# First groups transposed on TensorE, one softmax for both ends, and a new planner cost, in a dynamic convolution with Fourier mixing and an MLP

## The chip, the cores and the metric

The kernel runs on one NeuronCore of a Trainium2 chip. The metric is the time of one execution on the device, in microseconds (us). Five engines work beside each other, each in its own order: PE (TensorE, matrix products), DVE (VectorE), ACT (ScalarE), POOL (GpSimd) and SP (SyncE, which here issues all transfers). An instruction waits at the head of its engine until what it needs is there, and everything behind it on that engine waits with it.

## The reference

The input x has 8 batches of 4224 positions with 192 channels; weight_gen has for each position 8 heads with 7 taps.

```python
w = softmax(weight_gen, axis=-1)                      # with 1e-9 in the sum
x_pad = zeros of 6 positions in front of x
c[b, s, head] = sum_k w[b, s, head, k] * x_pad[b, s + k, head]   # 24 channels a head
u = c + real(fft(fft(c, axis=1), axis=2))
un = (u - mean(u)) / sqrt(var(u) + 1e-6)              # over the channels
out = u + relu(un @ w_ch1) @ w_ch2                    # 192 -> 768 -> 192
```

## The kernel before

The 4224 positions of a batch lie as 128 partitions by 33 rows; the host puts them in an order in which the transform along the sequence splits in a DFT of 128 and one of 33. Each batch goes through these stages.

- **conv**: softmax of the taps (`softmax_taps`, L503 to L515: load, maximum, subtraction, Exp on ACT, sum, reciprocal), weights made of it (wp, L604), products of x with the weights by chunk c of four rows, 0 to 8 (DVE at L673 `pr<-x_sb,wp`, POOL at L671, in batch 0 some on ACT at L641), and their sums: on PE by a matmul with the identity for some chunks of batch 0 (L679, L650), on POOL else (L683 `u<-u,pr`). Batches 0 and 1 make the softmax in three parts, rows 0 to 4, rows 29 to 32 and the middle.
- **transform**: POOL folds mirrored rows (sm, L697 and L699), PE makes the DFT of 128 (pg, L704), DVE gathers (gt, L711, L714), the result goes to DRAM (g_d) and comes back in another order (g, L739), PE makes the DFT of 33 (pp, L749), ACT copies it to pq (L753 to L763).
- **mix**, by group g of four rows, 0 to 8: PE makes the transform along the channels (eo, L778), ACT copies one half (ot, L783), DVE adds it to u (L784 to L788).
- **norm**: mean and variance (groups 0 to 2 of batch 0, the `QUICK` ones, by DVE at L812; else by ACT at L817, L819), the root on ACT (L821), the normalized un (ACT, L830), which is split into two fp16 parts hl (cast on ACT at L838, remainder at L839 and L841 on DVE for quick groups, on POOL else), and a DMA transpose of hl to ht (L847).
- **mlp**, numbered 0 to 71 over all batches: 30 fp16 matmuls `ph<-ht` (L872) with the two parts of w1, relu (ACT, with DVE at L883), then `po<-hh` (L895, f32 for the first 7 groups, three fp16 terms afterwards), addition to u (L900) and the output.

w1 and w2 arrive as wide words and are turned to f32 by seven DVE steps a part (L430 to L441, prep_w1, prep_w2), then split (split_f32).

The code lists these streams in a rough order (`add`, `queue`, `held`), and `plan()` then sets the order of every engine for the whole program: it walks the instructions with a cost for each (`cost()`), a time between engines (`HOP`), the Exp and Sqrt table load on ACT, and the buffers that come free, and keeps the best of several walks. Tiles of one tag share buffers in turn: "ph" has 3 banks of PSUM, "po" has 2, ht has 3 buffers in SBUF. `held(ins)` puts the instructions written in it behind `ins`.

`keep_warm` (L726) issues matmuls whose result nobody reads, so that PE isn't idle: 20 behind the last pg of batch 0 (warm_pp), 12 on hl_0 (warm_hl), 12 ahead of the MLP of group 1 (`late_warm`).

## Time and profile before

| what | before |
|---|---|
| runs | 1120.19, 1113.48, 1117.24 us; median 1117.24 |
| profiled execution | 1118.23 us, its span 1116.5 us |
| granted TensorE clock, mean | 0.989 of full |
| PE busy | 1072.5 us, 96% of the span |
| DVE, POOL, ACT busy | 964.1, 875.8, 820.4 us |
| moved by DMA | 128.71 MB, mean 115 GB/s |

Times in the profile run from the start of the span. A row of the timeline has the start, the length, the engine, the line of the kernel, the operation, and what it writes and reads; a bracket at the end is the idle time of the engine just before, and what ended it. Rows of matmuls count passes: an f32 matmul is two records. A DMA row on SPq is the issue alone.

### The profile page before, as it was taken

The page shows a single profiled execution, that of the slowest core. Times are in us where ns is not written, and L with a number is a line of the kernel's source. Part 1 is how long each engine was busy: PE and PEld are TensorE (multiplying, and loading weights), DVE is VectorE, ACT ScalarE, POOL GpSimd, SP SyncE. Part 2 cuts the span into 40 slices and gives each one's busy share as a digit, 9 for nine tenths or more (in the row PEclk, how much of TensorE's full clock was granted, in tenths as well). Part 3 has the DMA queues.
Part 4 walks back from the last instruction along what each step waited for, and adds up shares of the span by engine and source line. Part 5 has one row for each costly group of instructions (what it writes and reads, how often), then busy time and mean ns, then how long its engine had stood idle before and what let it go on. Part 6 is the DMA issues. An engine that isn't in the chain of part 4 may idle for free.

```text
span 1116.5 us, 23468 instructions
## 1 busy us (share of the span) xinstructions
PE 1072.5 (96%) x8476; PEld 822.3 (74%) x8476; DVE 964.1 (86%) x1773; ACT 820.4 (73%) x2415; POOL 875.8 (78%) x759
## 2 busy tenths in 40 slices
PE   5885999999989999999999999999999999999998
PEld 3464687887768877777778877787778777886777
DVE  7988998889979999999989999999989998355543
ACT  4665666769866887878797878778787878689832
POOL 5979799799959999599969999599969999111200
PEclk9997999999999999999999999999999999999999
DMA  9354136514464246624454337614543322613221
GB/s 319 122 154 113 36 115 188 140 40 135 124 171 105 79 121 196 146 66 121 114 169 104 93 108 212 145 48 124 128 136 103 72 61 71 146 44 75 72 48 47
DMA packets 156500, 128.71 MB, mean 115 GB/s; under 512 B 108571, under 2 KB 133088, under 8 KB 156384
## 3 DMA queue, kind: packets, MB, share of 16 engines
q1 hardware_dynamic: 156384, 127.21, 42.6%
q8 instruction: 67, 1.10, 0.4%
q14 instruction: 49, 0.40, 0.1%
HBM read 61.46 MB, written 39.37 MB: 90 GB/s over the span
## 4 chain that ended last, share of the span: by engine, by line
PE 66%; POOL 10%; DVE 9%; issue 5%; DMA 3%; ACT 2%; SPq 0%; DVEq 0%; ACTq 0%; POOLq 0%
PE ph L872 28%; PE po L895 26%; POOL u L683 8%; PE pp L749 5%; PE eo L778 4%; DVE pr L673 3%; PE pg L704 2%; DMA g<-g_d 1%; DVE hh L883 1%; POOL sm L697 1%; PE pa L679 1%; DMA ht<-hl 1%; DMA g_d<-gt 1%; ACT un L830 1%; DVE u L673 1%
## 5 line engine op out<-in xcount | busy, mean ns | idle before, releaser
L683 POOL TENSOR_TENSOR u<-u,pr 128x768 f32<-128x768 f32 (+1 forms) x396 | 654.9, 1675 | 20.3 <-DVE pr L673 9.5
L895 PE MATMUL po<-w2h,hh 128*128 128x192 f16 x2832 | 421.9, 246 | 0.1
L895 PEld LDWEIGHTS <-hh 128*128 128x128 f16 x4248 | 364.8, 98 | 70.0 <-issue 0.6
L872 PE MATMUL ph<-ht,w1h 128*128 128x512 f16 (+1 forms) x1296 | 400.9, 363 | 6.8 <-DMA ht<-hl 3.9
L673 DVE TENSOR_TENSOR pr<-x_sb,wp 128x768 f32<-128x768 f32 (+1 forms) x415 | 356.2, 880 | 21.7 <-POOL u L683 19.3
L895 PE MATMUL po<-w2l,hh 128*128 128x192 f16 x1416 | 348.3, 246 | 0.0
L883 DVE SCALAR_TENSOR_TENSOR hh<-ph,hh 128x512 f16<-128x512 f32 (+1 forms) x390 | 247.9, 638 | 80.2 <-ACT hh L882 79.6
L872 PE MATMUL ph<-ht,w1l 128*128 128x512 f16 (+1 forms) x864 | 311.4, 363 | 0.0
L882 ACT ACTIVATE hh<-ph 128x512 f16<-128x512 f32 (+1 forms) x390 | 214.8, 551 | 121.5 <-PE ph L872 94.4
L872 PEld LDWEIGHTS <-w1h 128*128 128x128 f16 x1296 | 126.3, 99 | 88.3 <-DMA ht<-hl 3.5
L830 ACT ACTIVATE un<-u,rs 128x192 f32<-128x192 f32 x264 | 127.6, 536 | 31.5 <-POOL rs L828 23.3
L839 POOL TENSOR_TENSOR hl<-un,hl 128x512 f16<-128x512 f32 (+1 forms) x69 | 74.3, 1076 | 70.0 <-ACT hl L838 36.1
L872 PEld LDWEIGHTS <-w1l 128*128 128x128 f16 x864 | 85.7, 99 | 44.6 <-issue 3.0
L819 ACT ACTIVATE junk<-u,st 128x192 f16<-128x192 f32 x252 | 113.6, 451 | 4.1
L817 ACT ACTIVATE junk<-u 128x192 f16<-128x192 f32 x252 | 90.6, 360 | 22.7 <-DVE u L788 19.1
L778 PE MATMUL eo<-cs_sb,pq 97*128 97x97 f32 x544 | 88.1, 271 | 2.1 <-DVE u L788 1.9
L778 PEld LDWEIGHTS eo<-cs_sb,pq 97*128 97x128 f32 x544 | 81.9, 191 | 11.1 <-issue 2.1
L900 DVE SCALAR_TENSOR_TENSOR u<-po,isc,u 128x384 f32<-128x384 f32 (+1 forms) x122 | 73.0, 598 | 10.8 <-PE po L895 10.6
L828 POOL TENSOR_TENSOR rs<-st,rs 128x4 f32<-128x4 f32 (+1 forms) x69 | 13.8, 202 | 80.9 <-DVE rs L822 76.8
L697 POOL TENSOR_TENSOR sm<-u 128x382 f32<-128x382 f32 x64 | 64.5, 1008 | 4.0 <-ACT u L692 4.0
L753 ACT COPY pq<-pp 97x204 f32<-97x204 f32 (+1 forms) x96 | 46.4, 484 | 26.3 <-PE pp L749 21.7
L895 PE MATMUL po<-w2f,hh 128*128 128x192 f32 x336 | 64.3, 328 | 0.0
(108 smaller groups left out, 1291.2 us busy)
## 6 DMA issues: line engine op xcount, KB each, us to landing
out_dram<-u SPq DMA_DIRECT2D x64, 384.0 KB
x_sb<-in_x_dram SPq DMA_DIRECT2D x48, 384.0 KB
g<-g_d SPq DMA_DIRECT2D x40, 336.0 KB
x_sb<-in_x_dram SPq DMA_DIRECT2D x8, 864.0 KB
g_d<-gt SPq DMA_DIRECT2D x32, 195.0 KB
g_d<-gt SPq DMA_DIRECT2D x32, 189.0 KB
w<-in_weight_gen_dram SPq DMA_DIRECT2D x6, 924.0 KB
x_sb<-in_x_dram SPq DMA_DIRECT2D x8, 672.0 KB
```

The lines of the kernel that those rows point to most:

```text
L673: last_product[b] = nc.vector.tensor_tensor(out=dst, in0=rows, in1=wk, op=ALU.mult)
L683: adder.tensor_tensor(out=u, in0=u, in1=pr, op=ALU.add)
L697: nc.gpsimd.tensor_tensor(out=sm[:, :, 1:D], in0=u[:, 0:2, 1:D], in1=u[:, 3:1:-1, D - 1:0:-1], op=ALU.add)
L778: nc.tensor.matmul(eo[:, e, j, :], lhsT=pq[0:DH, e, r, r:r + P], rhs=cs_sb[:, e, :], start=True, stop=True)
L817: nc.scalar.activation(junk, uv[:, t, :], AF.Identity, scale=-1.0 / D, accum_out=st[:, t, 0:1])
L819: nc.scalar.activation(junk, uv[:, t, :], AF.Square, bias=st[:, t, 0:1], accum_out=st[:, t, 1:2])
L830: nc.scalar.activation(halves[t // 2][:, t % 2, :], uv[:, t, :], AF.Identity, bias=rs[:, 1, t:t + 1], scale=rs[:, 0, t:t + 1])
L839: lo_eng.tensor_tensor(out=hl[:, t0:t1, 2 * P:3 * P], in0=src[:, 0:t1 - t0, 0:P], in1=hl[:, t0:t1, 0:P], op=ALU.subtract)
L872: last_ph[n] = nc.tensor.matmul(ph[:, 0:T], lhsT=wt[:, cs_], rhs=ht[:, 0:T, blk], start=(i == 0), stop=(i == len(terms) - 1))
L882: nc.scalar.activation(a[:, 0:T], ph[:, 0:T], AF.Relu)
L883: nc.vector.scalar_tensor_tensor(out=l[:, 0:T], in0=ph[:, 0:T], scalar=0.0, in1=a[:, 0:T], op0=ALU.max, op1=ALU.subtract)
L895: nc.tensor.matmul(po[t // 2][:, t % 2, :], lhsT=hx[:, t], rhs=wx[:, c2, :], start=(c2 == 0 and i == 0), stop=(c2 == NH - 1 and i == len(t ...
```

## The change

1. **Softmax of batches 0 and 1.** Rows 0 to 4 and 28 to 32 are loaded by one mirrored DMA and go through one set of operations (128x2x280), the middle has 1288 elements instead of 1344. In batch 0 the middle's sums get a copy of row 28 to 32's part.
2. **Loads at the start.** SP issues the softmax's ends first, then x of 1344 columns; a memset of a column of x_sb is placed on DVE behind the first softmax reduction, so that the next x load (384), and by `holds` everything behind it on SP, waits for DVE.
3. **Quick groups.** For groups 0 to 2 of batch 0 the halves of un in PSUM and hl go; un lies in SBUF, eight f32 matmuls with the identity transpose it into two "po" banks (tr), ACT casts to ht, DVE subtracts for the remainder. Three DMA transposes go.
4. **Warm-ups.** 14 matmuls on the identity at the start, 40 behind conv(0)'s last chunk, 8 behind the mix of group 1 and 8 behind that of group 2; warm_hl and late_warm go.
5. **Root.** One Sqrt on a constant (`root`) behind the last pq copy makes ACT load its table there.
6. **Order of the start.** mix and norm of groups 0 to 2 are written interleaved; prep_w2(0) and (1) use "ph" banks and come behind the first split of w1, prep_w2(2) is queued at group 1.
7. **plan().** A transfer's cost has a third term, its load on one shared wire, by which the end of each transfer is moved back behind the earlier ones; the cost of a run of bytes and of a transpose is set anew. `HOP` keeps its values and `SLACK` is 0.

The core of the diff:

```diff
-WARM = (20, 0, 12, 12)
+WARM = {-1: 14, 7: 40}
+WARM_EO = (8, 8)
...
         if ins.opcode == "DmaTransposeAnt":
-            return 1450, 2000 + 1.2 * n
-        return 400, 2000 + WIRE * count(out) * BYTES[out.dtype]
+            return 1450, 2000 + 1.2 * n, 1.09 * n
+        size, run = BYTES[out.dtype], min(together(ap) for ap in reads + writes)
+        return 400, 2000 + WIRE * count(out) * size, out.ap[0][1] * count(out) / run * (0.5 + 0.0023 * run * size)
...
-            busy, done = ops[k][2]
+            busy, done, *load = ops[k][2]
             free[lane], end = now + busy, now + done
+            if load and not back:
+                wire = max(wire, now + 1000) + load[0]
+                end = max(end, wire + 1000)
...
-        parts = [(0, 5), (29, N2), (5, 29)] if b < 2 else [(0, N2)]
+        parts = [(-1, 5), (5, N2 - 5)] if b < 2 else [(0, N2)]
...
-            need_x(0)
-            tap_step(0, 7)
+            with held(loads[0].ins):
+                need_x(NC)
+            with held(tops[0].ins):
+                nc.vector.memset(x_sb[:, 7:37:29, 0:1], 0.0)
+            first = len(nc.cur_bb.bb.instructions)
+            need_x(0)
+            holds.append((first + 1, 1e9, nc.cur_bb.bb.instructions[first]))
+            tap_step(0, 4)
...
+            ht = sb.tile([P, 4, 3, P], F16, tag="ht", name=f"ht_{b}_{g}", bufs=3)
+            tr = [pst("po", 2, [P, 4, P], F32, f"tr_{b}_{g}_{i}") for i in range(2)]
+            R = D - P
+            for i, m in ((0, P), (1, R)):
+                for t in range(T):
+                    nc.tensor.matmul(tr[i][0:m, t, :], lhsT=un[:, t, i * P:i * P + m], rhs=ident32, start=True, stop=True)
+                nc.scalar.copy(ht[0:m, 0:T, i], tr[i][0:m, 0:T])
+                at = P - m
+                last_lo[NG * b + g] = nc.vector.tensor_tensor(out=ht[at:P, 0:T, 2 - i], in0=tr[i][0:m, 0:T],
+                                                              in1=ht[0:m, 0:T, i], op=ALU.subtract)
...
-    with held(last_pg[0].ins):
-        WARM[0] and keep_warm(("po", 2), "pp", ident32, last_tile[0][:, 3, 0:P], WARM[0])
+    with held(last_pq[0].ins):
+        nc.scalar.activation(sb.tile([P, D], F16, tag="junk", name="root", bufs=2)[:, 0:1], eps_t, AF.Sqrt)
...
-    for i in range(2):
-        queue(last_split[-1].ins, (prep_w2, i))
+    for i in range(2):
+        queue(last_split[0].ins, (prep_w2, i))
```

What this makes of the engines' orders, at three places. In these rows the line numbers of the new kernel are its own: its L872 is the transposing matmul, L917 the old L872, L875 the subtraction, L892 the old L847, L541 to L547 the softmax (L505 to L515), L713 the old L673, L822 to L826 the mix.

PE at the start of the first MLP, before (ht_0 is the transposed activations of group 0, ph_0_0 the first part of its hidden layer):

```order
121 L726 MATMUL warm_hl_988<-hl_0_981 128x384
122 L726 LDWEIGHTS hl_0_981
123 L726 MATMUL warm_hl_988<-hl_0_981 128x384
124 L872 LDWEIGHTS w1h_87
125 L872 MATMUL ph_0_0_1108<-ht_0_1001,w1h_87 128x512
126 L872 LDWEIGHTS w1l_88
127 L872 MATMUL ph_0_0_1108<-ht_0_1001,w1l_88 128x512
128 L872 LDWEIGHTS w1h_87
```

and now:

```order
108 L872 MATMUL tr_0_0_1013<-ident_72,un_0_965 128x128
109 L872 MATMUL tr_0_1_1014<-ident_72,un_0_965 64x128
110 L872 MATMUL tr_0_0_1013<-ident_72,un_0_965 128x128
111 L872 MATMUL tr_0_1_1014<-ident_72,un_0_965 64x128
112 L917 LDWEIGHTS w1h_87
113 L917 MATMUL ph_0_0_1152<-ht_0_1012,w1h_87 128x512
114 L917 LDWEIGHTS w1l_88
115 L917 MATMUL ph_0_0_1152<-ht_0_1012,w1l_88 128x512
116 L917 LDWEIGHTS w1h_87
117 L917 MATMUL ph_0_1_1160<-ht_0_1012,w1h_87 128x512
118 L917 LDWEIGHTS w1l_88
119 L917 MATMUL ph_0_1_1160<-ht_0_1012,w1l_88 128x512
```

The MLP's first matmul stood behind the warm-up on hl_0 and waited for a DMA transpose; now it stands behind tr, the transposes by matmul, and after two matmuls PE goes over to ph_0_1.

DVE at the end of the softmax of batch 1's middle, before (wp is its tile, hl_2 the fp16 parts of group 2, w2f and its temporaries the conversion of w2):

```order
222 L515 RECIPROCAL wp_799<-wp_799 128x192
223 L436 TENSOR_SCALAR pa_w_2_1095<-pw_w_2_1096 128x384
224 L604 TENSOR_TENSOR wp_799<-w_800,wp_799 128x224
225 L439 SCALAR_TENSOR_TENSOR t_w_2_1097<-raw_w_419,pa_w_2_1095 128x384
226 L673 TENSOR_TENSOR u_2_1361<-x_sb,wp_799 128x768
227 L673 TENSOR_TENSOR pr_2_1_1364<-x_sb,wp_799 128x768
228 L673 TENSOR_TENSOR pr_2_2_1377<-x_sb,wp_799 128x768
229 L683 TENSOR_TENSOR u_2_1361<-u_2_1361,pr_2_1_1364 128x768
230 L441 TENSOR_TENSOR w2f<-pw_w_2_1096,t_w_2_1097 128x384
231 L673 TENSOR_TENSOR pr_2_3_1385<-x_sb,wp_799 128x768
232 L784 TENSOR_TENSOR eo_3_1132<-eo_3_1132,ot_3_1155 128x2x97
```

and now:

```order
212 L545 TENSOR_REDUCE wp_831<-w_832 128x184
213 L546 TENSOR_SCALAR wp_831<-wp_831 128x184
214 L547 RECIPROCAL wp_831<-wp_831 128x184
215 L751 TENSOR_TENSOR gt_0_1221<-pg_0_1218,up_79 128x2x97
216 L644 TENSOR_TENSOR wp_831<-w_832,wp_831 128x224
217 L754 TENSOR_TENSOR gt_0_1221<-pg_0_1218,up_79 128x2x95
218 L713 TENSOR_TENSOR u_2_1392<-x_sb,wp_831 128x768
219 L713 TENSOR_TENSOR pr_2_1_1395<-x_sb,wp_831 128x768
220 L713 TENSOR_TENSOR pr_2_2_1408<-x_sb,wp_831 128x768
221 L723 TENSOR_TENSOR u_2_1392<-u_2_1392,pr_2_1_1395 128x768
222 L713 TENSOR_TENSOR pr_2_3_1416<-x_sb,wp_831 128x768
223 L856 RECIPROCAL rs_3_1249<-rs_3_1249 128x4
```

The sum (L510 before, L545 now) and all behind it have moved behind the two subtractions of ht_2, which wait for ACT, and behind the mix of group 3; the conversion of w2 has moved ahead of them.

SP in batch 1, before (ht_4 is group 4's transposed activations, x_sb and w the loads for the next batch, g_d the write of the transform):

```order
114 L717 DMA g_d_95<-gt_4_2925 65x768
115 L718 DMA g_d_95<-gt_4_2925 63x768
116 L904 DMA out_dram<-u_1_841 128x768
117 L556 DMA x_sb<-in_x_dram 128x768 x3
118 L556 DMA x_sb<-in_x_dram 128x576
119 L503 DMA w_5465<-in_weight_gen_dram 128x1848
120 L847 DMA_TRANSPOSE ht_4_3092<-hl_4_3088 128x12x128
121 L904 DMA out_dram<-u_2_1361 128x768
```

and now:

```order
104 L949 DMA out_dram<-u_0_843 128x768
105 L892 DMA_TRANSPOSE ht_4_3123<-hl_4_3119 128x12x128
106 L586 DMA x_sb<-in_x_dram 128x768 x2
107 L949 DMA out_dram<-u_1_866 128x768
108 L757 DMA g_d_95<-gt_4_2956 65x768
109 L758 DMA g_d_95<-gt_4_2956 63x768
110 L586 DMA x_sb<-in_x_dram 128x768 x3
111 L586 DMA x_sb<-in_x_dram 128x576
112 L539 DMA w_5496<-in_weight_gen_dram 128x1848
113 L949 DMA out_dram<-u_2_1392 128x768
114 L892 DMA_TRANSPOSE ht_5_3321<-hl_5_3317 128x12x128
```

The transpose of ht_4 has moved ahead of five x loads and of the w load; the transpose of ht_5 now follows that w load.

More of the change, by code (lines that the diff above doesn't have):

```diff
@@ L113, in covers, with together @@
     return len(sa) == 1 and pa[0] <= pb[0] and pb[1] <= pa[1] and sa[0][0] <= sb[0][0] and sb[-1][1] <= sa[0][1]
+def together(ap):
+    run = 1
+    for step, n in reversed(ap.ap[1:]):
+        if n > 1 and step != run:
+            break
+        run *= n
+    return run
 def cost(ins, lane, reads, writes):
@@ L188, in walk @@
         free, waiting = {lane: 0.0 for lane in HOP}, {lane: set() for lane in HOP}
-        order, table = {lane: [] for lane in HOP}, None
+        order, table, wire = {lane: [] for lane in HOP}, None, 0.0
         for k, n in enumerate(left):
@@ L232, in walk @@
                 loose = lanes[j] == lane and (lane == "pe" or not sync)
-                ready[j] = max(ready[j], now if loose else end + HOP[lane if back else lanes[j]])
+                ready[j] = max(ready[j], now if loose else end + HOP[lane if back else lanes[j]] + (SLACK if lanes[j] != lane else 0))
                 left[j] -= 1
@@ L486, in split_w2, with mirrored, keep_warm @@
         nc.vector.tensor_tensor(out=isc, in0=scales[0][:, 1:2], in1=s2[:, 1:2], op=ALU.mult)
-    wbanks = {}
+    def mirrored(ap, step):
+        return bass.AP(ap.tensor, ap.offset, [ap.ap[0], [step, 2], *ap.ap[1:]])
+    def keep_warm(spare, count):
+        for _ in range(count):
+            nc.tensor.matmul(spare, lhsT=ident32, rhs=ident32, start=True, stop=True)
+    wbanks, loads, tops = {}, [], []
     def softmax_taps(b, parts):
@@ L720, in conv @@
                 yield done / N2
-    def keep_warm(bank, nm, lhsT, rhs, count):
-        spare = pst(*bank, [P, 512], F32, f"warm_{nm}")
-        for _ in range(count):
-            nc.tensor.matmul(spare[:, 0:rhs.shape[-1]], lhsT=lhsT, rhs=rhs, start=True, stop=True)
+            if b == 0 and WARM.get(grp[0]):
+                with held(last_pg[0].ins):
+                    keep_warm(pst("po", 2, [P, P], F32, f"warm_{grp[0]}"), WARM[grp[0]])
     def transform(b):
@@ L956, in tile_dynconv_fnet_mlp, with step @@
             break
-    tap8, tap9 = ((lambda n: tap_step(1, n), n) for n in (8, 9))
+    tap8, tap9 = ((lambda n: tap_step(1, n), n) for n in (5, 6))
     queue(lp, (prep_w1, loaded[0]))
-    for i in range(2):
-        queue(last_split[-1].ins, (prep_w2, i))
-    for g in range(QUICK):
-        add(0.0, 1.0, behind(last_split[-1].ins, mix(0, g)))
-        run()
-        add(0.0, 1.0, norm(0, g))
-        run()
-    for g, call in ((0, tap8), (1, (prep_w2, 2)), (1, tap9)):
+    mixes, norms = ([f(0, g) for g in range(QUICK)] for f in (mix, norm))
+    def step(gen, n=99):
+        for _, at in zip(range(n), gen):
+            pass
+    step(mixes[0])
+    step(norms[0], 1)
+    warm = pst("po", 2, [P, P], F32, "warm_eo")
+    for g in range(1, QUICK):
+        step(mixes[g], 4)
+        with held(last_mix[0].ins):
+            keep_warm(warm, WARM_EO[g - 1])
+    step(norms[0])
+    for i in range(2):
+        queue(last_split[0].ins, (prep_w2, i))
+    for g in range(1, QUICK):
+        step(mixes[g])
+        step(norms[g])
+        if g == 1:
+            queue(last_split[0].ins, (prep_w2, 2))
+    for g, call in zip(TAPS_AT, (tap8, tap9)):
         queue(last_lo[g].ins, call)
```

115 lines of the change are left out of this document (60 added, 55 removed).

## The prediction

> **What bounds the kernel now.** I read the page first, then the table of stretches, then PE's waits behind its first MLP matmul, and last the timeline of the places that these named. Of the page, the shares of the chain that ended last:
>
> ```profile
> PE 66%; POOL 10%; DVE 9%; issue 5%; DMA 3%; ACT 2%; SPq 0%; DVEq 0%; ACTq 0%; POOLq 0%
> ```
>
> PE carries 66% of it and POOL 10%. The stretches (us, then busy time and number of instructions of each engine; PEclk is the granted clock):
>
> ```profile
> core 0: us, PE busy (x) PEld busy (x) DVE busy (x) ACT busy (x) POOL busy (x), PEclk, DMA share, GB/s
> 95.00:113.60 18.60, 7.07 (x40) 4.53 (x38) 16.73 (x64) 10.61 (x25) 18.60 (x12) 0.72 0.12 23
> 113.60:126.00 12.40, 12.39 (x58) 6.74 (x59) 11.27 (x21) 7.38 (x13) 4.91 (x7) 0.86 0.34 65
> 126.00:200.00 74.00, 71.72 (x409) 56.75 (x408) 67.95 (x119) 50.32 (x146) 73.37 (x59) 1.00 0.47 129
> 311.00:319.00 8.00, 4.75 (x30) 3.15 (x28) 5.01 (x8) 3.87 (x9) 4.70 (x6) 0.79 0.88 252
> 319.00:1117.00 798.00, 792.69 (x6810) 615.33 (x6807) 676.61 (x1216) 607.86 (x1747) 595.16 (x529) 1.00 0.41 105
> ```
>
> From 319 to the end PE is busy for 792.69 of 798.00 us: little is to be gained there, so a change pays only where PE stands idle or runs at a lower clock. There are three such places. Before 113.6 it waits for a serial start: of 18.60 us it works 7.07. In 113.6 to 126 its clock is 0.86, and in 311 to 319 it is busy for 4.75 of 8.00 us at a clock of 0.79. What PE waits for from 113 us on (us in total, times, longest):
>
> ```profile
> PE ph L872 <- DMA ht<-hl: 3.9, 2, 3.3
> PE ph L872 <- DVE hl L841: 2.5, 1, 2.5
> PE pg L704 <- POOL sm L699: 1.8, 1, 1.8
> ```
>
> The 3.3 us belong to one group's transposed activations, ht_4 of batch 1, and make the hole at 311; the 2.5 us are the end of the wait for the very first ht. The forecast is thus about two places, the road to the first MLP matmul and that hole, and about whether the new order makes holes of its own.
>
> A measurement of this kernel can tell about 0.5% from no change, 5.6 us: faster means under 1111.65 us, slower over 1122.8. The profiled execution took 1118.23 us (span 1116.5), 1.0 above the median of the runs shown.
>
> **The change, part by part.** *Start of conv(0).* One softmax of 560 elements takes the place of two. The first product of 768 columns was:
>
> ```profile
> 9.56 2.60 DVE L673 TENSOR_TENSOR pr<-x_sb,wp 128x768 f32<-128x768 f32 x5
> ```
>
> With one load and one set of five operations the weights come some 1.5 us earlier (an estimate: half of the operations ahead of 9.56 go), but the x rows for this product are now held behind the first reduction, and all loads behind them on SP start later by about 0.9. I take the product at 9.0 (9.0 to 10.0). The loads' delay is met again later in conv(0), so the end of conv(0) moves by 0 (-0.5 to +1.0).
>
> *First transform.* The matmuls that keep the clock up, and a wait behind them:
>
> ```profile
> 72.66 6.36 PE L726 MATMUL warm_pp<-gt,ident 128*128 128x128 f32 x40 [0.40 <-DVE gt L714]
> ...
> 89.02 0.91 PE L749 MATMUL pp<-te_sb,g 102*97 102x102 f32 x8 [2.50 <-DMA g<-g_d]
> ```
>
> 40 passes (20 matmuls) took 6.36 us, partly at half clock. Now 40 matmuls, 80 passes, stand in this place: at most 12.7 us by this row, and near 9 at full clock, so the second DFT (pp) may begin up to 2 us later. But its third g load (the 2.50) lets PE wait until 89.02 in any case, and hides this. Cost 0; without that cover, up to 2 us.
>
> *From the last pq copy to the first MLP matmul.* ACT's rows of before:
>
> ```profile
> 100.83 1.28 ACT L821 ACT_TABLE_LOAD   x1
> 102.12 0.30 ACT L821 ACTIVATE rs<-st,eps_t 128x4 f32<-128x4 f32 x1
> 103.58 1.82 ACT L830 ACTIVATE un<-u,rs 128x192 f32<-128x192 f32 x4 [1.16 <-DVE rs L825]
> 105.34 0.84 ACT L838 CAST hl<-un 128x384 f16<-128x384 f32 x2
> ```
>
> and the rows of SP and PE behind them:
>
> ```profile
> 107.39 16.28 SPq L847 DMA_TRANSPOSE ht<-hl  x3
> ...
> 107.47 3.63 PE L726 MATMUL warm_hl<-hl 128*128 128x384 f16 x12 [7.07 <-DVE rs L822]
> ...
> 113.61 0.10 PEld L872 LDWEIGHTS <-w1h 128*128 128x128 f16 x1 [2.90 <-DVE hl L841]
> ...
> 122.58 2.11 PE L726 MATMUL warm_hl<-hl 128*128 128x384 f16 x12
> ```
>
> The Sqrt table load moves ahead of the first ot copy. That copy, and with it the mix, comes some 0.7 us later; the 1.28 between the statistics and Sqrt goes. un begins near 102.8 instead of 103.58 and ends 1.8 later, at 104.6. Before, a cast (0.84 for two halves), DVE's subtractions and a DMA transpose stood behind it: issued at 107.39, its ht let PE go at 113.61, 6.2 us for the transpose alone. Now eight f32 matmuls with the identity follow un row by row. A pass took 0.16 us in the 6.36 us row and near 0.11 at full clock; a matmul has two passes. Only the last pair stands behind un: 0.7. Then one cast of 512 columns, 0.6 (0.42 for 384 by the row at 105.34). The MLP starts at about 106.05: **-7.5** (-8 to -6).
>
> The Trainium skill, page "ScalarE: Activation LUTs", section "What ACT_TABLE_LOAD costs", gives 2.66 us for each switch, a drain of 1.38 included. The trace differs: Sqrt starts at 102.12, right behind the load of 1.28, and no drain stands between them. By the page's figure the moved load would gain 1.38 more where it goes and cost ot_0 1.38 more where it comes, and the sum would be the same within 1 us.
>
> *Work that PE gains and loses.* The transposes of groups 1 and 2 lie behind the first MLP matmul: 16 matmuls, 32 passes at 0.11, 3.6 us. The 12 matmuls at 122.58 (2.11) go. **+1.5.** The clock: in 113.6 to 126 PE lost 12.40 x 0.14 = 1.7 us to it. Before that PE had been idle for 7.07 us (the row at 107.47) and then for 2.51. Now 16 extra matmuls stand between the mixes of groups 0 to 2, the transposes follow, and no gap is over 3 us; I take **-1.7** (0 if the clock stays low).
>
> The Trainium skill, page "TensorE: Matmul & The Clock Gate", section "HAM oscillation — how this bites in real kernels", says that PE gaps of over some 3.4 us bring the throttle back; the trace agrees, with 0.72 in 95 to 113.6. Its section "Part 4: PE-mode transpose" speaks against this change, for transposes in that mode don't count as busy. These are ordinary matmuls with an identity, so I hold it unlikely here; it is the clock rival below.
>
> *New waits in the first two groups.* On ACT the copy of ot_3 now stands ahead of the first relu, and the Exp of batch 1's softmax with its table load (1.28, as above) and two casts of ht_2 stand ahead of the relus of hh_0_4 and hh_0_5. PE waits for a free ph bank: about 1.2 before ph_0_3 (a copy and a relu at 0.6 each), and about 1.0 behind the Exp. tr_2 takes a po bank that DVE's conversion of w2's third part holds, and DVE has much queued ahead of the end of that. DVE's groups in 107 to 126 (count | busy, mean ns of one):
>
> ```profile
> L510 DVE TENSOR_REDUCE wp<-w 128x192 f32<-128x1344 f32 x1 | 1.6, 1562 | 0.5 <-ACT w L508 0.5
> L506 DVE TENSOR_TENSOR w<-w,wp 128x1344 f32<-128x1344 f32 x1 | 1.5, 1546 | 0.0
> L505 DVE TENSOR_REDUCE wp<-w 128x192 f32<-128x1344 f32 x1 | 1.5, 1530 | 0.0
> L841 DVE TENSOR_TENSOR hl<-un,hl 128x128 f16<-128x128 f32 x5 | 1.4, 282 | 0.0
> L515 DVE RECIPROCAL wp<-wp 128x192 f32<-128x192 f32 x1 | 1.4, 1355 | 0.0
> ```
>
> ht_1's last subtraction ends near 111.2 by the same reckoning; behind it come a reduction (1530 ns) and a subtraction (1546) of the softmax, seven conversion steps of under 0.5 and four steps of the mix, 8.0 us in all: 119.2. PE would be there at 117.3: about 1.8. All are estimates from these rows: **+4.0** (+2 to +6). So MLP group 1 starts -7.5 + 1.5 - 1.7 + 4.0 = 3.7 us earlier than before.
>
> *Who comes late behind this.* The softmax of batch 1's middle now ends behind the subtractions of ht_2, which wait for tr_2. Before, DVE's first product of conv(1)'s chunk 2, and POOL's addition behind it:
>
> ```profile
> 122.10 0.95 DVE L673 TENSOR_TENSOR u<-x_sb,wp 128x768 f32<-128x768 f32 x1
> ...
> 125.72 3.72 POOL L683 TENSOR_TENSOR u<-u,pr 128x768 f32<-128x768 f32 x2 [7.49 <-DVE u L683]
> ```
>
> Now: 119.2, tr_2 1.8, cast 0.6, two subtractions 1.2, sum 1.56, reciprocal 1.36, two or three short steps 1.0: 126.7 instead of 122.10. POOL starts 4.6 later than 125.72, and cannot make it up: it is busy for 73.37 of 74.00 us until 200. How near is it to PE?
>
> ```profile
> 197.98 0.19 POOL L699 TENSOR_TENSOR sm<-u 128x2 f32<-128x2 f32 x1
> ...
> 205.08 0.81 PE L704 MATMUL pg<-sm,f_sb 128*128 128x192 f32 x4
> ```
>
> sm_7 is ready at 198.17 and PE uses it at 205.08: 6.9 us in hand. A lead of 3.7 on PE and a delay of 4.6 on POOL make 8.3. The row of additions ahead of sm_7 has lost one hl (about 1.8) and gained one short addition, so 0.7 of the lead goes and **-3.0** stays (0 to -3.7). At chunk 5, where PE waited 1.8 for sm, the new order puts sm_5 ahead of four additions of 1.8, which pays for the delay there.
>
> *The hole at 311.* SP's rows, and the transpose in the chain:
>
> ```profile
> 303.11 3.13 SPq L556 DMA_DIRECT2D x_sb<-in_x_dram  x4
> 306.39 0.33 SPq L503 DMA_DIRECT2D w<-in_weight_gen_dram  x1
> 307.32 4.04 SPq L847 DMA_TRANSPOSE ht<-hl  x1
> ```
>
> ```profile
> 307.32 7.89 DMA ht<-hl
> ```
>
> Four x loads and a w load were issued just ahead; the transpose of ht_4 behind them landed 7.89 us after its issue. In the new order this transpose stands ahead of those loads, and the two halves of its hl are adjacent on POOL. The wait of 3.3 goes, and the low clock behind it (8.00 x 0.21 = 1.7). What is late next is PE's own work. I take **-4.5** (-5.0 to 0).
>
> *The rest.* The planner's new transfer backlog moves thousands of instructions. From 319 on PE stands idle for 5.3 us in all, so there is little to win, and any burst of loads can be put badly: **+1** (-2 to +4).
>
> Sum: -3.0 - 4.5 + 1.0 = -6.5. From 1118.23 that is 1111.7, from the median 1110.7; I say **1111.0**.
>
> **The rivals.** *POOL eats the start.* conv(1) hangs on POOL, as the chain's 10% says. If its additions slip by 8 us instead of 4.6, the lead is spent, and -4.5 + 1.0 = -3.5 remains: 1113.7. For it: POOL is full from 126 to 200; against: 6.9 us in hand.
>
> *The hole is only moved.* ht_5 now stands behind the w load instead of ht_4. If it is caught in the same way, the 4.5 are lost: -3.0 + 1.0, 1115.2.
>
> *Slower: bursts ahead of transposes in several batches.* A transpose issued within a microsecond of a w load (306.39 and 307.32) cost 3.3 + 1.7 = 5.0 us. In most batches the new SP order has ht_5 close behind x and w loads. Three hits decide it: -3.0 - 4.5 + 15 = +7.5, 1124.7. Against: before, other batches had such neighbours too, and PE's list of waits has one long wait for ht only.
>
> *The clock stays low at the first MLP matmuls.* The 1.7 is not won and the last transposes take 0.4 longer: -6.5 + 2.1 = -4.4, 1112.8.
>
> **How the numbers follow.** The forecast has 0.55 (its own spread is 1104 to 1115; 0.47 lies under 1111.65 and 0.08 above), POOL 0.14, the moved hole 0.13, the low clock 0.06, the bursts 0.12. Faster: 0.47, and 0.04 from the good ends of the others, 0.51. Slower: 0.10 of the bursts and 0.02 of others, 0.12. Same: 0.37. The range's low end has the good ends of the start, the hole and the rest (-3.7 and 2 more, -5.0, -2, with the runs' spread some -14): 1103. Its high end takes in two hits and the start lost, 1121; a third hit is left out.
>
> **What would show it.** Right: the first MLP matmul near 106, group 1 near 123; clock near 1 from there; POOL's first addition of conv(1)'s chunk 2 near 130, and under 1 us of PE waits for it; no long wait for ht at 300 to 320. Wrong: a first MLP matmul behind 109; PE waiting several us for POOL's sm or for ht between 185 and 265; waits of 3 us for ht in later batches, with a low clock behind each.

## The result, and the profile after

The changed kernel takes 1108.39 us in the median of 5 runs (1106.92 to 1108.77), the kernel before 1118.6 (1113.48 to 1120.7): a ratio of 0.9908, with a 95% interval from 0.9888 to 0.9928, so 10.2 us faster. The forecast was 1111.0 in a range of 1103 to 1121. The profiled execution took 1108.65 us, its span is 1106.7.

Of its page, the shares of the chain that ended last:

```profile
PE 76%; DVE 8%; POOL 5%; issue 4%; DMA 4%; ACT 3%; SPq 0%; DVEq 0%; POOLq 0%; ACTq 0%
```

PE has gone from 66% to 76%, POOL from 10% to 5%. The table of stretches shows where, in the columns of before:

```profile
core 0: us, PE busy (x) PEld busy (x) DVE busy (x) ACT busy (x) POOL busy (x), PEclk, DMA share, GB/s
...
95.00:106.00 11.00, 9.86 (x65) 7.34 (x64) 10.22 (x45) 5.49 (x13) 11.00 (x8) 1.00 0.00 0
106.00:113.60 7.60, 6.69 (x37) 3.81 (x38) 6.45 (x16) 4.64 (x11) 7.52 (x7) 1.00 0.01 2
113.60:126.00 12.40, 12.32 (x75) 9.52 (x74) 11.71 (x20) 11.40 (x30) 1.98 (x3) 1.00 0.00 0
126.00:200.00 74.00, 70.25 (x396) 54.96 (x395) 68.24 (x118) 45.93 (x134) 73.29 (x58) 1.00 0.42 127
...
311.00:319.00 8.00, 8.00 (x63) 5.45 (x62) 7.27 (x11) 2.39 (x4) 8.00 (x12) 1.00 1.03 230
319.00:1107.00 788.00, 782.03 (x6728) 606.51 (x6725) 671.11 (x1211) 602.07 (x1737) 591.03 (x521) 1.00 0.41 106
```

Before, PE worked 7.07 of the 18.60 us up to 113.6, and 4.75 of the 8.00 us from 311; now it works 16.55 of the 18.60 and all of the 8.00, and the clock, which was 0.72, 0.86 and 0.79 in the three stretches, is 1.00 in every row. What PE waits for from 60 us on (us in total, times, longest):

```profile
PE ph L917 <- DMA ht<-hl: 2.9, 3, 1.4
PE pg L744 <- POOL sm L739: 2.3, 3, 1.4
PE me_w L432 <- DVE m_w L430: 1.5, 1, 1.5
PE ph L917 <- ACT hh L923: 0.9, 1, 0.9
PE pp L786 <- DMA g<-g_d: 0.9, 1, 0.9
```

No wait is over 1.5 us, where one of 3.3 and one of 7.07 stood before. The road to the first MLP matmul, in PE's timeline:

```profile
71.78 8.08 PE L514 MATMUL warm<-ident 128*128 128x128 f32 x70
...
86.72 0.91 PE L786 MATMUL pp<-te_sb,g 102*97 102x102 f32 x8 [0.85 <-DMA g<-g_d]
...
92.01 2.26 PE L816 MATMUL eo<-cs_sb,pq 97*128 97x97 f32 x16
94.10 1.98 PE L514 MATMUL warm_eo<-ident 128*128 128x128 f32 x16
...
99.82 3.19 PE L872 MATMUL tr<-ident,un 128*128 128x128 f32 x16 [0.28 <-ACT un L862]
103.32 0.38 PE L917 MATMUL ph<-ht,w1h 128*128 128x512 f16 x1 [0.31 <-ACT ht L873]
...
111.19 0.38 PE L917 MATMUL ph<-ht,w1h 128*128 128x512 f16 x1 [0.91 <-ACT hh L923]
```

and in ACT's:

```profile
92.65 1.28 ACT L996 ACT_TABLE_LOAD   x1
...
98.31 0.30 ACT L855 ACTIVATE rs<-st,eps_t 128x4 f32<-128x4 f32 x1 [0.18 <-DVE st L847]
99.22 1.86 ACT L862 ACTIVATE un<-u,rs 128x192 f32<-128x192 f32 x4 [0.61 <-DVE rs L860]
...
102.68 1.06 ACT L873 CAST ht<-tr 128x512 f16<-128x512 f32 x2 [1.42 <-PE tr L872]
```

The first MLP matmul starts at 103.32 instead of 113.61, 10.3 us earlier; the un operations start at 99.22 instead of 103.58, and between un and the MLP lie 4.10 us instead of 10.03. At the second place, SP's rows:

```profile
289.58 1.44 SPq L892 DMA_TRANSPOSE ht<-hl  x1
...
301.87 4.80 SPq L586 DMA_DIRECT2D x_sb<-in_x_dram  x4
306.77 0.38 SPq L539 DMA_DIRECT2D w<-in_weight_gen_dram  x1
...
309.69 3.80 SPq L892 DMA_TRANSPOSE ht<-hl  x1
```

The transpose of ht_4 (289.58) goes ahead of the burst of x and w; that of ht_5 (309.69) is caught behind it, and PE works through.

Where the same matmul stands in both traces gives the course of the lead (start of the n-th record of that form, from both timelines):

| record | before | after | lead |
|---|---|---|---|
| first mix matmul (eo) | 95.12 | 92.01 | 3.1 |
| 1st MLP record (ph) | 113.61 | 103.32 | 10.3 |
| 361st, ahead of the hole | 298.77 | 292.26 | 6.5 |
| 421st, behind the hole | 330.39 | 318.21 | 12.2 |
| 601st | 411.97 | 401.07 | 10.9 |
| 2101st of 2160 | 1091.40 | 1081.80 | 9.6 |

Between these records the orders differ, and the lead swings with them: it is 2.9 at the 181st record and 8.1 at the 301st. The last one is nearly the difference of the spans (9.8).

### The profile page after: what moved, and what is told of

Its sections match the earlier page's. It is cut to its first block, busy times and chain, and to the rows that moved or that the text cites. A ratio compares the mean times of both kernels' runs of the same rounds, so it can differ in the third digit from the quotient of the medians.

```text
span 1106.7 us, 23668 instructions
## 1 busy us (share of the span) xinstructions
PE 1083.5 (98%) x8600; PEld 832.6 (75%) x8600; DVE 964.0 (87%) x1759; ACT 817.6 (74%) x2414; POOL 876.7 (79%) x759
## 4 chain that ended last, share of the span: by engine, by line
PE 76%; DVE 8%; POOL 5%; issue 4%; DMA 4%; ACT 3%; SPq 0%; DVEq 0%; POOLq 0%; ACTq 0%
PE ph L917 32%; PE po L940 29%; PE pp L786 5%; PE eo L816 5%; DVE pr L713 4%; POOL u L723 3%; PE pg L744 3%; DMA ht<-hl 2%; PE warm L514 1%; PE tr L872 1%; DMA x_sb<-in_x_dram 1%; POOL sm L737 1%; DVE u L723 0%; DVE u L713 0%; ACT w L543 0%
## 5 line engine op out<-in xcount | busy, mean ns | idle before, releaser
L917 PE MATMUL ph<-ht,w1h 128*128 128x512 f16 (+1 forms) x1296 | 397.8, 362 | 4.2 <-DMA ht<-hl 2.9
L713 DVE TENSOR_TENSOR pr<-x_sb,wp 128x768 f32<-128x768 f32 (+1 forms) x415 | 355.6, 878 | 15.5 <-POOL u L723 13.3
L917 PE MATMUL ph<-ht,w1l 128*128 128x512 f16 (+1 forms) x864 | 310.2, 362 | 0.0
L917 PEld LDWEIGHTS <-w1h 128*128 128x128 f16 x1296 | 125.4, 98 | 87.3 <-DMA ht<-hl 3.1
L882 ACT ACTIVATE un<-u,rs 128x192 f32<-128x192 f32 x252 | 121.3, 538 | 23.3 <-POOL rs L880 19.5
L917 PEld LDWEIGHTS <-w1l 128*128 128x128 f16 x864 | 85.3, 99 | 44.7 <-issue 2.3
L816 PE MATMUL eo<-cs_sb,pq 97*128 97x97 f32 x544 | 82.5, 272 | 0.8 <-DVE u L826 0.5
L816 PEld LDWEIGHTS eo<-cs_sb,pq 97*128 97x128 f32 x544 | 77.9, 192 | 7.2 <-issue 0.9
```

The lines of the kernel that those rows point to most:

```text
L713: last_product[b] = nc.vector.tensor_tensor(out=dst, in0=rows, in1=wk, op=ALU.mult)
L816: last_mix[b] = nc.tensor.matmul(eo[:, e, j, :], lhsT=pq[0:DH, e, r, r:r + P], rhs=cs_sb[:, e, :], start=True, stop=True)
L882: nc.scalar.activation(un[:, t, :], uv[:, t, :], AF.Identity, bias=rs[:, 1, t:t + 1], scale=rs[:, 0, t:t + 1])
L917: last_ph[n] = nc.tensor.matmul(ph[:, 0:T], lhsT=wt[:, cs_], rhs=ht[:, 0:T, blk], start=(i == 0), stop=(i == len(terms) - 1))
```

## The experiments

Each kernel is planned anew by its own planner after its edit, so an edit can move other rows as well; where the traces show that, it is said. The times stand beside runs of the kernel before on the same chip, whose median lay between 1117.86 and 1118.88.

### The hole, put right in the kernel before

```diff
 order = best[2]
+sp, pl = order["sp"], order["pool"]
+at = next(i for i, ins in enumerate(sp) if name(ins).startswith("ht_1_4"))
+sp.insert(at - 5, sp.pop(at))                 # ht_4 of batch 1 ahead of five loads
+a, b = (i for i, ins in enumerate(pl) if name(ins).startswith("hl_1_4"))
+pl.insert(a + 1, pl.pop(b))                   # its hl's second half behind the first
```

> The kernel before with two moves in its finished order and nothing else: in batch 1 the transpose of ht_4 stands ahead of the last three x loads of 768, the x load of 576 and the w load, and the second half of its hl stands right behind the first on POOL. Theory of two places: the hole at 311 to 319 goes, PE waits less than 0.5 us there at full clock, and the time falls by 4 to 5 us against before, to 0.996. Rival, that the hole only covers what PE would have waited for next (POOL's additions or a later transpose): a fall of less than 1.5 us, with new waits of 2 to 4 us by 340.

Measured: 1114.24 us (1110.82 to 1119.34, 12 runs), a ratio of 0.9963 [0.9944, 0.9981], 4.1 us faster. The stretch of the hole in its trace:

```profile
311.00:319.00 8.00, 8.00 (x67) 5.81 (x65) 7.41 (x11) 6.05 (x16) 8.00 (x10) 1.00 0.63 229
```

PE works all of the 8.00 us at full clock, instead of 4.75 at 0.79. Its lead over before goes from 0.6 at the 361st MLP record to 5.4 at the 421st, and 4.4 are left at the 2101st. The edit makes two moves, and the trace of before shows that SP's place alone would not have done it: the second half of this group's hl stood late on POOL and ended at 307.30, and the transpose was issued at 307.32.

```profile
306.61 0.69 POOL L841 TENSOR_TENSOR hl<-un,hl 128x256 f16<-128x256 f32 x1
```

With both moves it is issued at 302.09. The two together are worth some 4 us, kept to the end.

### The hole, put back into the changed kernel

```diff
 order = best[2]
+sp = order["sp"]
+at = next(i for i, ins in enumerate(sp) if name(ins).startswith("ht_1_4"))
+w = next(i for i in range(at, len(sp)) if name(sp[i]).startswith("w_"))
+sp.insert(w, sp.pop(at))                      # ht_4 behind the w load
```

> The changed kernel with one move in its finished order: in batch 1 the transpose of ht_4 goes behind the w load that it now stands ahead of. Theory of two places: PE waits for ht near 305 to 316, some 5 to 10 us, with half clock behind, and the changed kernel loses 5 to 11 us, so that most or all of its gain is gone. Rival, that the place of this transpose is not what brought the second half of the gain: a loss under 2 us.

Measured: 1120.86 us (1116.98 to 1122.95, 11 runs), ratio 1.0019 [1.0003, 1.0034]: 12.5 us over the changed kernel, and the whole gain gone. Its SP rows, and PE's wait:

```profile
301.58 4.80 SPq L591 DMA_DIRECT2D x_sb<-in_x_dram  x4
306.47 0.38 SPq L544 DMA_DIRECT2D w<-in_weight_gen_dram  x1
307.02 2.56 SPq L897 DMA_TRANSPOSE ht<-hl  x1
```

```profile
314.33 0.61 PE L922 MATMUL ph<-ht,w1h 128*128 128x512 f16 x1 [8.69 <-DMA ht<-hl]
```

The transpose is issued at almost the same time as in before (307.02, there 307.32) and holds PE until 314.33, but PE has been ready since 305.64, as it is earlier by then: a wait of 8.69 us instead of 3.3. In this traced execution, the fastest of the eleven, that costs 8.3 us to the end; the median has 12.5, at mean clocks of 0.989 to 0.995, so that the half clock behind such a wait is the likely rest. A transfer that lands at a given time eats whatever lead came before it. So the two parts of the change aren't a sum: with the hole in place the start is worth nothing. With the hole out of the way it is worth more than was forecast: the changed kernel leads the kernel of the last experiment, which has the hole mended and the old start, by 5.2 to 6.2 us from the 541st MLP record on, and by 5.85 in the medians. The prediction had 3.0.

### The transposes by DMA again

```diff
-tr = [pst("po", 2, ...)]; 8 matmuls on ident32; cast to ht; subtract for the remainder
+hl = sb.tile([P, 4, 2 * D], F16, tag="hl", ...)
+nc.scalar.copy(hl[:, 0:T, 0:D], un); 2 subtractions on DVE; DMA transpose of hl to ht
```

> The changed kernel, but the three quick groups are transposed by DMA as before (cast to hl on ACT, remainder on DVE, DMA transpose of hl; no matmul with the identity); the rest, with the order of the start and the warm-ups, stays. Theory of two places: the first MLP matmul comes 5 to 7 us later than in the changed kernel, at 108 to 110; POOL has only some of that lead left by 210, so the whole loses 2 to 5 us against the changed kernel. Rival A, that POOL's chain of conv(1) swallows all of the lead: a loss under 1 us. Rival B, that the lead goes through whole: 6 to 7 us.

Measured: 1119.11 us (1117.52 to 1121.97, 12 runs), ratio 1.0007 [0.9992, 1.0021], 10.7 over the changed kernel. This run is not a clean test of the transpose, as one DVE row of its trace shows:

```profile
104.92 8.04 DVE L870 TENSOR_TENSOR hl<-un,hl 128x512 f16<-128x512 f32 x1
...
118.02 0.68 DVE L870 TENSOR_TENSOR hl<-un,hl 128x512 f16<-128x512 f32 x1
```

The same subtraction takes 0.68 us in one group and 8.04 in another, and the first MLP matmul waits for it until 118.81. So it was run once more with un in PSUM, as in the kernel before:

```diff
+if quick: halves = [pst("ph", 3, [P, 2, D], F32, ...) for i in range(2)]   # un in PSUM
```

> The changed kernel with the quick groups transposed by DMA, and un in PSUM halves as in the kernel before, so that DVE's remainder has one operand in PSUM. In the first try of this (un in SBUF) one DVE subtraction of 512 columns took 8.04 us beside a busy POOL, and that, not the transpose, made most of its loss. Theory of two places: without that the first MLP matmul comes 5 to 7 us later than in the changed kernel (108 to 110), and the time is 3 to 6 us over it. Rival A, that POOL's chain of conv(1) had swallowed the lead: under 1.5 us over it. Rival B, that the DVE stall was not the cause: again some 10 us over it, with the first matmul near 118.

Measured: 1114.79 us (1113.77 to 1118.14, 9 runs), ratio 0.9978 [0.9966, 0.9989], 6.4 over the changed kernel. Its PE:

```profile
100.21 1.98 PE L514 MATMUL warm_eo<-ident 128*128 128x128 f32 x16
115.36 0.61 PE L918 MATMUL ph<-ht,w1h 128*128 128x512 f16 x1 [13.18 <-DVE hl L874]
```

The subtractions are short again (0.41 at 104.78), the first group's transpose is issued at 108.30, and PE stands idle for 13.18 us. The first MLP matmul comes 12.0 later than in the changed kernel, of which 8.1 are left at the 61st record and 6.1 at the end. Not all of this is the transposes': the start was planned anew, and un comes 3.1 later already (102.36, not 99.22). From un to the first MLP matmul it is 13.0 us instead of 4.1.

### Without the warm-ups

```diff
-WARM = {-1: 14, 7: 40}
+WARM = {}
-        with held(last_mix[0].ins):
-            keep_warm(warm, WARM_EO[g - 1])
```

> The changed kernel without any of its matmuls for the clock (14, 40, 8 and 8 left out). If the clock is what they bring: half clock in a window of 3.4 us near 74 to 95 and again at the first MLP matmuls near 103, the first MLP matmul 1 to 2 us later, and a loss of 2 to 4 us in all. Rival, that the transposes, mixes and pp matmuls keep the clock up without them, or that the lead is lost behind POOL anyway: within 1 us of the changed kernel.

Measured: 1113.59 us (1112.22 to 1114.54, 11 runs), ratio 0.9957 [0.9943, 0.9972], 5.2 over the changed kernel.

```profile
81.61 1.65 PE L786 MATMUL pp<-te_sb,g 102*97 102x102 f32 x8 [8.42 <-issue]
...
104.20 5.46 PE L872 MATMUL tr<-ident,un 128*128 128x128 f32 x16 [1.81 <-ACT un L862]
```

Behind an idle time of 8.42 us the second DFT's rows take 1.65 instead of the 0.87 to 0.94 of the changed kernel, and the 16 transposing passes 5.46 instead of 3.19. The first mix matmul comes at 95.79, not 92.01, the first MLP matmul at 109.71, not 103.32. The clock in 73 to 95 is 0.69 and in 106 to 113.6 it is 0.53, where the changed kernel has 1.00. But conv(0) was planned anew as well: its last write of g_d is issued at 74.07 instead of 71.52, so 2.5 of the 3.8 us at the first mix matmul stand ahead of the second DFT. Matmuls that nobody reads are thus worth up to 5 us here; how much of it is the clock alone, this run can't say.

### Without the preloaded root

```diff
-    with held(last_pq[0].ins):
-        nc.scalar.activation(sb.tile([P, D], F16, tag="junk", name="root", bufs=2)[:, 0:1], eps_t, AF.Sqrt)
```

> The changed kernel without the Sqrt on a constant behind the last pq copy; the Sqrt table is loaded at the first root. Theory of the prediction's sum: the mix of group 0 begins 0.7 us earlier and the load of 1.28 us stands between the statistics and the root again, so the first MLP matmul comes 0.8 us later and the time rises by 0.5 to 1 us. Rival, that the load hides in ACT's wait for DVE's statistics: within 0.4 us. By the Trainium skill, page ScalarE: Activation LUTs, section What ACT_TABLE_LOAD costs, the switch has a drain of 1.38 us too, and the loss would be up to 2.2 us.

Measured: 1112.97 us (1111.66 to 1118.99, 12 runs), ratio 0.9956 [0.9941, 0.9972], 4.6 over the changed kernel. The profiled execution is the longest of the twelve, so its times after the start say little; in it ACT loads the table between the statistics and the root again:

```profile
101.62 1.28 ACT L855 ACT_TABLE_LOAD   x1
...
103.92 1.87 ACT L862 ACTIVATE un<-u,rs 128x192 f32<-128x192 f32 x4 [0.71 <-DVE rs L860]
```

A load of 1.28 us costs 4.6 in the median. The mean clock of the runs is 0.991 to 0.995, against 0.997 to 1.0 with the root; the traced execution has a half clock at 89.1 to 99.4 and 106.2 to 113.0. The first of these stretches begins ahead of the load, so the trace doesn't tie it to that. That the rest of the 4.6 is the clock is possible, but it wasn't tried apart from the load, and the cause stays open.

### The old start

```diff
-parts = [(-1, 5), (5, N2 - 5)] if b < 2 else [(0, N2)]
+parts = [(0, 5), (29, N2), (5, 29)] if b < 2 else [(0, N2)]      # and x's loads as before
```

> The changed kernel with the softmax of batches 0 and 1 in three parts and the loads ungated, as before. By the traces of the two kernels the last pg of conv(0) came 1.1 us earlier with the change, and the third g load let PE wait 1.7 us less. Theory that the start's softmax made this: the second DFT begins 0.5 to 1.1 us later than in the changed kernel and the time is 0.5 to 2.5 us over it. Rival, that this part is worth nothing (as forecast): within 0.5 us.

Measured: 1111.06 us (1109.16 to 1113.79, 5 runs), ratio 0.994 [0.9926, 0.9953], 2.7 over the changed kernel. Its second DFT starts 2.8 later in the traced execution, which is the longest of the five. The prediction had put the one softmax at 0.

### The new waits of the first groups, one by one

First the middle of batch 1's softmax placed earlier and later among the groups:

```diff
-TAPS_AT = (1, 2)
+TAPS_AT = (0, 1)
```

> The changed kernel with the two later steps of batch 1's softmax queued behind groups 0 and 1 instead of 1 and 2 (TAPS_AT), so that DVE ends this softmax ahead of ht_2's subtractions and POOL's additions of conv(1)'s chunk 2 begin some 2 to 4 us earlier than 126.6. Theory that POOL's chain takes a part of the lead: PE's waits for sm (2.3 us in all) go, and the time falls by 1 to 2.5 us against the changed kernel. Rival, that PE alone sets the end: within 0.7 us.

```diff
-TAPS_AT = (1, 2)
+TAPS_AT = (2, 2)
```

> The changed kernel with both later steps of batch 1's softmax queued behind group 2, so that POOL's additions of chunk 2 begin some 2 to 5 us later. Theory that POOL's chain binds: PE waits for sm longer by about that, and the time rises by 2 to 5 us. Rival, that POOL has some 7 us in hand and PE alone sets the end: within 0.7 us of the changed kernel.

Earlier: 1108.64 us (1106.97 to 1109.63, 4 runs), ratio 0.9914 [0.9901, 0.9928], no difference from the changed kernel. PE's waits for sm are gone from its list and others stand there (in all, eo for u 1.5, po for u 1.1, me_w for hh 1.0). Later: 1113.01 us (1111.49 to 1115.18, 5 runs), ratio 0.9954 [0.994, 0.9968], 4.6 slower. There POOL's first addition of conv(1)'s chunk 2 stands at

```profile
132.99 1.81 POOL L723 TENSOR_TENSOR u<-u,pr 128x768 f32<-128x768 f32 x1 [2.73 <-DVE u L723]
```

6.4 later than in the changed kernel (126.63). In its trace 2.4 of the 4.6 stand already at the first MLP matmul (a start that the planner laid otherwise), still 2.4 at the 61st, and 4.7 at the 241st. That the late POOL costs these 2.3 is not shown: PE's waits for sm are shorter there than in the changed kernel (1.6 in all, not 2.3). Longer are a wait for a relu (1.51, not 0.91) and the one for m_w on DVE (1.95, not 1.50), with a half clock at 190.2 to 193.7 behind it. Then PE's two longest waits of 160 to 190 us taken away by the order alone:

```diff
 order = best[2]
+for what, by in (("pg_1_4", 8), ("me_w2", 4)):       # PE takes these later
+    late = [ins for ins in pe if name(ins).startswith(what)]
+    at = pe.index(late[-1]) + 1 + by
+    pe[:] = [ins for ins in pe[:at] if ins not in late] + late + pe[at:]
```

> The changed kernel with two moves in its finished order on PE: the matmuls of pg of batch 1's chunk 4 eight instructions later (PE waited 1.44 us for POOL's sm there), and the matmul me_w2 of w2's scale four instructions later (PE waited 1.50 us for DVE). Theory that after the first MLP matmul PE's work alone sets the end, and each wait on PE is a pure loss: both waits shrink to under 0.5 us and the time falls by 1.5 to 2.5 us against the changed kernel. Rival, that POOL's chain of conv(1) sets it: the waits come again later (at other pg, at pp or at ht before 270), and the time stays within 0.7 us.

Measured: 1107.3 us (1106.6 to 1109.1, 5 runs), ratio 0.99 [0.9883, 0.9918], which holds the changed kernel's. Both waits (1.44 and 1.50) are gone, and at the next pg stands

```profile
180.74 0.92 PE L750 MATMUL pg<-sm,f_sb 128*128 128x192 f32 x4 [2.25 <-POOL sm L745]
```

Between the first and the 601st MLP record the trace gains nothing over the changed kernel (a lead of 0.7 and one of 0.5). Behind this wait the clock is half at 181.6 to 185.0. What PE doesn't wait at one pg it waits at the next, since POOL's additions set the pace there (73.29 of 74.00 us busy).

### The transfers ahead of the second DFT

```diff
-        with held(g2_loads[0, 2 * TRI].ins):
+        with held(last_g2[0].ins):               # w1's copies behind the last g load
```

> The changed kernel with the eight copies that spread w1's second half over the partitions (SP, 77.0 to 82.7 us) put behind the last g load of batch 0 instead of between the third and the fourth. Theory that SP's queue delays the g loads and with them the second DFT: the wait of pp for g (0.85 us) goes, the mix of group 0 begins 0.5 to 1.5 us earlier, and the time falls by 0.5 to 1.5 us. Rival, that the g loads wait for their buffers or for the DMA engines in any case: within 0.5 us; and if the copies then come too late for the MLP, a first MLP matmul later than 103.3 by a microsecond or more.

Measured: 1109.27 us (1107.25 to 1110.85, 6 runs), ratio 0.9917 [0.9898, 0.9935]: no difference. PE's wait for g (0.9) is gone, and the first mix matmul moves by 0.14 us. What is left in PE's list of waits there is ACT's pq copies (0.9 and 0.6 in all).

### The transposes alone, in the kernel before

```diff
+if quick:                        # un in SBUF, 8 matmuls with the identity, cast, remainder
+    tr = [pst("po", 2, [P, 4, P], F32, ...) for i in range(2)]
+    ...
-words_to_f32(loaded[1][i], w2_part(i)[0], f"w2_{i}", ("po", 2))
+words_to_f32(loaded[1][i], w2_part(i)[0], f"w2_{i}", ("ph", 3))
-    add(0.93, 0.95, late_warm(1))
```

> The kernel before with one part of the change alone: groups 0 to 2 of batch 0 keep un in SBUF and are transposed by f32 matmuls with the identity (tr, an ACT cast, a DVE remainder) instead of hl and a DMA transpose; the two warm-ups that hung on hl (12 matmuls on hl_0, 12 ahead of group 1) go, and w2's conversion takes ph banks. The softmax, the loads, the root and all other warm-ups stay as before. The planner, which is that of before, now puts the transpose of ht_4 of batch 1 ahead of the x loads and the w load by itself. Theory (the changed kernel's 10 us come from the transposes, 4 to 6 at the first MLP matmul, and from the transpose of ht_4 put ahead of the burst, 4 to 5; the root, the warm-ups and the softmax are each worth what their own runs showed): the first MLP matmul starts 4 to 6 us earlier than before's 113.61, because the Sqrt table load still stands in the way and the clock is still low ahead of it; the hole at 311 is gone; the time is 6 to 8 us under the kernel before. Rival 1 (the transposes alone carry nothing, only the hole counts): the first MLP matmul earlier or not, the time some 4 us under before. Rival 2 (the transposes are the whole start and warm-ups and root are decoration): first MLP near 104, the time 10 us under before, equal to the changed kernel.

Measured: 1127.06 us (1126.02 to 1128.22, 5 runs), ratio 1.0082 [1.0068, 1.0096]: 9.2 us slower than before. The theory and both rivals were wrong. PE's rows:

```profile
107.52 5.45 PE L836 MATMUL tr<-ident,un 128*128 128x128 f32 x16 [3.63 <-ACT un L827]
114.09 5.46 PE L836 MATMUL tr<-ident,un 128*128 128x128 f32 x16 [1.12 <-ACT un L827]
123.29 1.93 PE L836 MATMUL tr<-ident,un 128*128 128x128 f32 x5 [3.74 <-ACT un L827]
...
127.33 0.61 PE L883 MATMUL ph<-ht,w1h 128*128 128x512 f16 x1
```

and ACT's:

```profile
112.39 1.20 ACT L837 CAST ht<-tr 128x512 f16<-128x512 f32 x2 [3.61 <-PE tr L836]
113.49 1.42 ACT L827 ACTIVATE un<-u,rs 128x192 f32<-128x192 f32 x3
```

In this order the transposes of all three groups stand ahead of the first MLP matmul on PE, and the cast of one group ahead of the next group's un on ACT, so three groups pass one after another: un, tr, cast, un, tr, cast. PE pauses at each, its clock is 0.50 in the stretches from 106 to 126, and tr takes 5.45 instead of 3.19. A DMA transpose occupies none of these engines and let PE go over to the MLP of group 0; a transpose on PE is in the way of all that is queued behind it. The Trainium skill, page "VectorE: DVE Perf Modes", section "Rules for kernel authors", advises TensorE for a transpose of 128x128 where the result may lie in PSUM; the changed kernel agrees, this one shows that it depends on the order. The MLP starts at 127.33, 13.7 later than before, of which 3.3 stand already at un (106.92, before 103.58), as this kernel's start was planned anew too; at the hole, which this kernel's order lacks, 4.8 come back (a lag of 13.8 at the 361st record, 9.0 at the 421st). Which of the remaining parts makes the difference to the changed kernel, the root, the many warm-ups or the interleaved writing of the groups, this run can't say; without the root or without the warm-ups alone the changed kernel kept half of its gain.

### A finding from the orders

Planned with the old transfer cost, without the new backlog term, the changed kernel has the same order on all five engines, row for row, but for nine neighbouring small products on ACT. The kernel before with the new term has other rows, but its ht_4 of batch 1 stays behind the w load. So ht_4's place comes from the planning around the changed start, as it does in the last experiment, and the backlog term is worth nothing in this kernel.

## Why the prediction was right, and where it was not

- **The two places**: right. The wait for the first ht and the hole at 311 are gone, the clock is 1.00 behind both, and the rest of the program is as it was: from 319 on PE works 782.03 of 788.00 us, and had worked 792.69 of 798.00.
- **"the end of conv(0) moves by 0"** and **"its third g load lets PE wait until 89.02 in any case, and hides this"**: this step failed. PE passed at 86.72, with a wait of 0.85 instead of 2.50, and the first mix matmul came 3.1 earlier. The two traces split the 3.1 into three parts: the load of g was issued 0.8 earlier (82.80, not 83.58), it landed after 3.79 us instead of 5.30, which is 1.5, and the road behind it took 5.29 instead of 6.10, which is 0.8 and went at half clock for a stretch before. Ahead of the load conv(0) itself had moved, by 1.1 at its last write of g_d (71.52, not 72.63), where the prediction had 0. Why the load took longer before is open: its issue on SP took 1.62 us there and 0.52 in every other trace. A part is chance, too: the two traces of kernels that have before's order at the start put the first mix matmul at 95.12 and 93.62, and three that have the changed kernel's put it at 91.33 to 92.01. With the old start put back the 3.1 are gone (94.95), and without the warm-ups too (95.79), so neither holds them alone.
- **The road from the mix to the first MLP matmul, -7.5**: of the right kind. From the first mix matmul to un it is 1.25 shorter (the prediction: 0.8), from un to the MLP 5.9 (6.8): the transposing passes took 3.19 for 16, or 0.20 each, not 0.11. With the 3.1 ahead that makes the -10.3. So the mis-sized terms are the two zeros, for the end of conv(0) and for the first transform: together they measured 3.1 in these traces, and between 1.6 and 3.8 over the traces named.
- **The new waits, +4.0, and what POOL takes, 0.7**: from the first MLP record to the 361st the lead fell from 10.3 to 6.5, by 3.8, where the prediction had 7.5 to 3.0, so 4.5 with PE's own work and the clock in it. That the sum nearly came out is luck, for its parts did not. The relu ahead of ph_0_3 cost 0.91 (the prediction: 1.2), the transposes of groups 1 and 2 took 5.1 us (0.39 and 2.53, and 2.15), not 3.6, PE had no wait at tr_2, and POOL's first addition stood at 126.63, not at 130. The order itself was as forecast, as DVE's rows show (the fence on the new order begins one row behind the subtractions of ht_2):

```profile
117.42 0.69 DVE L875 TENSOR_TENSOR ht<-tr,ht 128x512 f16<-128x512 f32 x1 [0.40 <-ACT ht L873]
118.31 0.68 DVE L875 TENSOR_TENSOR ht<-tr,ht 64x512 f16<-64x512 f32 x1 [0.19 <-ACT ht L873]
118.92 1.48 DVE L545 TENSOR_REDUCE wp<-w 128x184 f32<-128x1288 f32 x1
```

  The sum starts at 118.92 where the prediction's reckoning gives some 122.8: its chain was laid on an MLP start of 106.05 and a wait of 1.8.
- **The hole, -4.5**: right, 4.1 in the kernel before, with ht_4's transpose and its hl both moved (4.4 in the trace). The sentence that hl's halves are adjacent on POOL was wrong, and ht_4 isn't held up by it. What the prediction lacked is the interplay: the price of the hole grows with the lead, 8.69 us of waiting instead of 3.3.
- **The rest, +1, from "the planner's new transfer backlog"**: the size fits (a lead of 10.9 at the 601st record and 9.6 at the end), the reason doesn't; the term changes nothing in the order but nine small products on ACT.
- **The sum, -6.5**: measured are -10.2 in the medians and -9.8 in the spans. The difference is the start, as the experiment on the hole in the kernel before shows: it brings some 5.5 us to the end, not 3.0. The median still lies 2.6 us from the forecast, well inside the range.
- **The rivals**: POOL eating the start was not reached; no run shows what such a delay would cost. The hole didn't move on to ht_5: it is caught behind the w load, but PE has other work then. Bursts in other batches: three waits for ht, 1.4 at most. The clock was at 1.00 from 14.7 us on: matmuls with the identity keep it up. The Trainium skill, page "TensorE: Matmul & The Clock Gate", section "Part 4: PE-mode transpose", says that transposes in that mode don't count as busy; no run here uses the mode, and the plain matmuls in its place counted.

Undone one at a time, the parts cost 6.4 (transposes, un in PSUM), 5.2 (warm-ups), 4.6 (root), 2.7 (start) and 12.5 (the place of ht_4): 31.4 for a change that brings 10.2, each with what its own planning moves. Done alone, ht_4's place with its hl brings 4.1 and the transposes lose 9.2. Prices of single edits, taken from runs like these, would thus not have given the result; the prediction's terms are steps of one chain through the new order, and could be added where no wait behind them takes the lead back.

## What to carry to other kernels

A serial start is one chain on one clock: follow the whole of it through the new order, including PE's pauses and what stands behind each instruction on its engine, and don't price its links apart. A transpose on PE instead of by DMA paid here where the order lets other work pass between its groups, and lost where it doesn't. A transfer queued behind a burst of loads can take back any lead that comes before it, so look at such places first, and judge a faster start only with them out of the way.
